# Normalised rows turned by transposing DMA on the sync queue instead of on TensorE

**Chip, cores, metric.** One core of one Trainium2 chip. The metric is the device time of one execution in microseconds (us), as the median of several runs. Runs are marked fast or slow by their state; only fast runs are compared.

## The reference

A block with two halves over 2048 rows of width 640. The first is an attention layer that works through segments of 32 rows, each preceded by 8 memory rows that are taken from the previous segment's own output, so the segments can't run side by side. The second is a feed-forward layer with a squared ReLU.

```python
def _A_ref(x, mem0, Wq, Wk, Wv, Wo, seg_len):
    mem = mem0
    for s in range(n_seg):                       # 64 segments, each needs the one before
        h = jnp.concatenate([mem, xs], axis=1)   # 8 memory rows + 32 rows of x
        q, k, v = (einsum('btd,dhe->bhte', h, W) for W in (Wq, Wk, Wv))   # 32 heads of 128
        p = _softmax(where(mask, q @ k * scale, -1e9))
        o = einsum('bhte,hed->btd', p @ v, Wo)
        mem = o[:, :M, :]
        outs.append(o[:, M:, :])

def _B_ref(x, w1, b1, w2, b2):                   # 640 -> 1728 -> 640
    r = relu(x @ w1 + b1)
    return (r * r) @ w2 + b2

h = x + _A_ref(_layernorm(x), ...)
return h + _B_ref(_layernorm(h), ...)
```

## The kernel before

The 64 segments are 16 blocks (128 rows each) of 4 steps. Between the pieces of a step's attention stand "fillers": units of the previous block's feed-forward and the tail projections of the next block. Rows are normalised in natural layout and then have to be turned, 128x640 in five 128x128 pieces, because the products that use them take them with the 640 along the partitions. Both turns are done on TensorE, with a copy out of PSUM on VectorE:

```python
def transposes(src):
    pt = mm.tile([128, DC, 128], BF16, tag="mm", name="pt")       # a bank of PSUM
    for c in range(DC):                                           # DC = 5
        nc.tensor.transpose(out=pt[:, c, :], in_=src(c), identity=ident)
    return pt

# norm_x: the rows of x, two blocks ahead
def turn():
    pt = transposes(lambda c: h["xn"][:, c * 128:(c + 1) * 128])
    ...
    def evac():                                                   # HT and hTt from pt, two copies
        nc.vector.tensor_copy(out=HT..., in_=pt[:, :, 0:96]...)
        nc.vector.tensor_copy(out=hTt[:], in_=pt[:, :, 96:128])
    late.append((0, evac))

# ffn: the rows that go into the feed-forward
def turn():
    pt = transposes(lambda c: h["hn"][:, c * 128:(c + 1) * 128])
    h["hnT"] = s1.tile([128, DC, 128], BF16, tag="hnT", name="hnT")
    late.append((0, lambda: nc.vector.tensor_copy(out=h["hnT"][:], in_=pt[:])))
    full.extend(...)                                              # its units may start
```

The turns are called in the middle of a step, ahead of the product O; `flush` first issues all the VectorE work that was put off. The end of a step is what the experiments turn on: SyncE issues the stores of the step's output rows (`keep`, "fo" in the profile), which wait for the copy `o`, and behind them the loads of feed-forward weights (`load_due`, "wf", 320 KB each, five buffers):

```python
def step(b, sp, fill):
    ...                                     # projections, scores, softmax sums, fillers
    if hturns:
        hturns.pop(0)()                     # step 2: the feed-forward's turn
    elif xturns:
        flush()                             # step 3: the turn of x
        xturns.pop(0)()
    pn = [normal(p[h], rz[h]) for h in range(2)]
    ...                                     # O, the copies oT, flush, fillers
    run_side()                              # parts of the normalising of later rows
    run_side()
    ...
    pw = bank(0, "pw")
    wo_units(lambda s: oT[s // 8][:, s % 8, TL:NQ], pw, slots_all)
    o = s2.tile([128, DG], BF16, tag="o", name="o")
    nc.scalar.copy(out=o[:], in_=pw[:, 0:DG])
    keep(o, b, sp * HD, M)                  # four stores on SyncE, they wait for o
    load_due()                              # three or four wf loads on SyncE
```

## Time and profile before

| | before |
|---|---|
| time | 1026.19 us, median of 3 (1025.86 to 1026.44) |
| span of the profiled run | 1027.4 us, mean granted clock 0.987 |
| TensorE busy | 952.6 us, 93% |
| VectorE / ScalarE / GpSimd busy | 516.3 / 434.8 / 161.3 us |
| step 3, blocks 2 to 14, in all | 198.9 us, TensorE idle for 12.8 of it |

Step lengths in this text are the distances between starts of the copy `o` from `pw` on ScalarE; there are 64 of them. A step runs from the copy of the step before it to its own copy, so fo and the wf loads that the program issues at the end of step 2 stand at the start of step 3 here. "Step 3" of a block is its fourth step. The prediction shows how the rest was read. Two lines of the waits view that it does not show are needed later (columns: engine, what waited, releaser; total us, times, longest us). The second is from the waits of SyncE's queue.

```profile
PE psf L355 <- DMA wf<-in_wf_dram: 3.4, 6, 1.1
```

```profile
SPq L300 <- ACT o L532: 282.1, 48, 12.0
```

TensorE waited little for feed-forward weights (psf is the feed-forward's "up" product). SyncE waited 282 us for the copies `o`: it had always got to the stores before the rows were there.

### The profile page before, as it was taken

How to read it: one execution, taken by the hardware profiler on the slowest of the kernel's cores; microseconds unless marked ns; L12 is line 12 of the kernel's file. 1: busy time of each engine (PE TensorE's matmuls, PEld its weight loads, DVE VectorE, ACT ScalarE, POOL GpSimd, SP SyncE). 2: the span in 40 equal slices, each digit the busy share in tenths (PEclk: the TensorE clock that was granted, in tenths of full speed). 3: DMA queues.
4: the chain of work that ended last, by engine and by line, in shares of the span. 5: the costliest groups of instructions: out<-in, count | busy, mean ns of one | idle time of the engine just before them, and what ended most of it. 6: DMA issues, size and time to landing. Idle time of an engine off the chain costs nothing.

```text
span 1027.4 us, 58454 instructions
## 1 busy us (share of the span) xinstructions
PE 952.6 (93%) x27584; PEld 624.4 (61%) x25755; DVE 516.3 (50%) x1362; ACT 434.8 (42%) x1084; POOL 161.3 (16%) x464
## 2 busy tenths in 40 slices
PE   2589889999999999999999999999999999999886
PEld 0155556666666756667675666667666666676454
DVE  2124355555645545564554556455555645555452
ACT  1144354444434443444445344444444444354331
POOL 0000101212120211212021121202112120301220
PEclk9979999999999999999999999999999999999998
DMA  9930002323422433242233424323342433234451
GB/s 352 423 143 22 19 16 70 105 87 102 129 76 83 118 107 102 86 129 82 80 116 105 125 64 129 101 86 90 106 126 64 129 102 94 75 112 121 152 174 63
DMA packets 74120, 114.70 MB, mean 112 GB/s; under 512 B 35344, under 2 KB 41616, under 8 KB 71440
## 3 DMA queue, kind: packets, MB, share of 16 engines
q1 hardware_dynamic: 73152, 110.60, 33.2%
q8 instruction: 208, 3.41, 1.4%
q10 hardware_dynamic: 720, 0.37, 0.1%
q14 instruction: 40, 0.33, 0.1%
HBM read 101.79 MB, written 6.55 MB: 105 GB/s over the span
## 4 chain that ended last, share of the span: by engine, by line
PE 84%; DMA 9%; DVE 3%; issue 2%; ACT 2%; POOL 1%; SPq 1%; POOLq 0%; DVEq 0%
PE ps L220 20%; PE ps L212 19%; PE pw L292 15%; PE pst L202 11%; PE psy L397 6%; PE psf L355 5%; DMA wf<-in_wf_dram 4%; PE pwt L292 3%; DMA wv<-in_wv_dram 2%; PE O L506 2%; DMA wk<-in_wk_dram 1%; DVE r L372 1%; PE pz L471 1%; PE A L457 1%; DMA wq<-in_wq_dram 1%
## 5 line engine op out<-in xcount | busy, mean ns | idle before, releaser
L428 ACT CAST row<-ps 128x512 bf16<-128x512 f32 x256 | 136.9, 586 | 153.4 <-PE ps L220 150.0
L220 PEld LDWEIGHTS <-HT 128*32 128x32 bf16 x3840 | 112.4, 97 | 120.3 <-issue 28.3
L292 PE MATMUL pw<-wo,oT 128*32 128x160 bf16 x8192 | 161.7, 237 | 10.4 <-issue 9.8
L292 PEld LDWEIGHTS <-oT 128*32 128x32 bf16 x8192 | 146.2, 99 | 34.7 <-ACT oT L517 20.8
L429 DVE STREAM_TRANSPOSE qT<-row 128x512 bf16<-128x512 bf16 x128 | 83.5, 690 | 128.5 <-ACT row L428 128.5
L212 PEld LDWEIGHTS <-HT 128*32 128x32 bf16 x2054 | 89.3, 97 | 73.0 <-issue 0.3
L220 PE MATMUL ps<-wq,HT 128*32 128x512 bf16 x1280 | 128.1, 381 | 0.8 <-DVE HT L195 0.8
L220 PE MATMUL ps<-wk,HT 128*32 128x512 bf16 x1280 | 128.0, 379 | 0.0
L212 PE MATMUL ps<-wk,HT 128*32 128x512 bf16 x1280 | 128.0, 379 | 0.0
L220 PE MATMUL ps<-wv,HT 128*32 128x512 bf16 x1280 | 127.7, 379 | 0.0
L212 PE MATMUL ps<-wv,HT 128*32 128x512 bf16 x1280 | 127.6, 379 | 0.0
L212 PE MATMUL ps<-wq,HT 128*32 128x512 bf16 x1280 | 127.4, 379 | 0.0
L520 POOL COPY oTt<-oT 128x64 bf16<-128x64 bf16 x256 | 49.5, 236 | 485.9 <-ACT oT L517 485.9
L429 DVE STREAM_TRANSPOSE kT<-row 128x512 bf16<-128x512 bf16 x128 | 83.5, 690 | 76.9 <-ACT row L428 76.9
L381 POOL TENSOR_TENSOR f1T<-r 128x256 bf16<-128x256 bf16 x93 | 57.7, 628 | 282.6 <-DVE r L372 131.5
L244 ACT CAST row<-pst 128x512 bf16<-128x512 f32 x96 | 56.2, 585 | 66.5 <-PE pst L202 56.9
L517 ACT CAST oT<-O 128x320 bf16<-128x320 f32 x128 | 48.3, 428 | 80.2 <-PE O L511 80.2
L202 PEld LDWEIGHTS <-hTt 128*32 128x32 bf16 x1920 | 47.4, 99 | 53.7 <-issue 29.9
L372 DVE TENSOR_SCALAR r<-psf,b1f 128x128 bf16<-128x128 f32 x218 | 66.2, 345 | 24.8 <-PE psf L355 15.9
L355 PE MATMUL psf<-hnT,wf 128*128 128x128 bf16 x1050 | 73.1, 219 | 5.1 <-DMA wf<-in_wf_dram 3.4
L532 ACT CAST o<-pw 128x160 bf16<-128x160 f32 x64 | 18.7, 292 | 137.0 <-PE pw L292 137.0
L519 DVE CAST oT<-O 128x320 bf16<-128x320 f32 x128 | 56.9, 486 | 39.1 <-PE O L511 39.1
(71 smaller groups left out, 1281.1 us busy)
## 6 DMA issues: line engine op xcount, KB each, us to landing
wf<-in_wf_dram SPq DMA_DIRECT2D x204, 320.0 KB
wq<-in_wq_dram SPq DMA_DIRECT2D x5, 1024.0 KB
wk<-in_wk_dram SPq DMA_DIRECT2D x5, 1024.0 KB
wv<-in_wv_dram SPq DMA_DIRECT2D x5, 1024.0 KB
wo<-in_wo_dram SPq DMA_DIRECT2D x4, 1280.0 KB
wq<-in_wf_dram SPq DMA_DIRECT2D x14, 320.0 KB
fo<-o SPq DMA_DIRECT2D x256, 7.5 KB
vturn<-row SPq DMA_DIRECT2D x120, 32.0 KB
```

The source lines that it names most:

```text
L202: nc.tensor.matmul(ps[32 * g:32 * g + 32, :], lhsT=lhs(c), rhs=w[:, c, g * EG + n * 512:g * EG + (n + 1) * 512], start=(c == 0), stop=(c = ...
L212: return te.add_instruction(mybir.InstMatmult(name=nc.get_next_instruction_name(), ins=[te.lower_ap(rhs), te.lower_ap(lhsT, for_matmul_wei ...
L220: (partial(again, g) if n else nc.tensor.matmul)(ps[n][32 * g:32 * g + 32, :], lhsT=lhs(c), rhs=w[:, c, g * EG + n * 512:g * EG + (n + 1) ...
L244: nc.scalar.copy(out=row[:], in_=st["ps"][:])
L292: nc.tensor.matmul(ps[32 * g:32 * g + 32, 0:DG], lhsT=lhs(s), rhs=wo[:, s, g * DG:(g + 1) * DG], start=(s == slots_all[0]), stop=(s == slo ...
L355: nc.tensor.matmul(ps[:, u * 128:(u + 1) * 128], lhsT=wfv[:, u, c], rhs=h["hnT"][:, c, :], start=(c == 0), stop=(c == DC - 1), skip_group_ ...
L372: nc.vector.tensor_scalar(out=r[0:fs, u, :], in0=src, scalar1=bias, scalar2=0.0, op0=ALU.add, op1=ALU.max)
L381: (nc.gpsimd if b < NB - 1 or k % 2 else nc.vector).tensor_tensor(out=f1T[:, 2 * k:2 * k + 2, :], in0=r[:], in1=r[:], op=ALU.mult)
L397: nc.tensor.matmul(h["ps"][:, 0:320], lhsT=f1T[:, fc + i, :], rhs=wf[:, (m % 4) * 320:(m % 4 + 1) * 320], start=(fc + i == 0), stop=(fc + ...
L428: nc.scalar.copy(out=row[:], in_=ps[n][:])
L429: nc.vector.transpose(out=dst(n), in_=blocks(row))
L519: nc.vector.tensor_copy(out=dst, in_=src)
```

## The change

The intent: take 145 turning instructions and the VectorE copies behind them off the busy engines, let idle SyncE and the DMA do the turn, and drop the flush ahead of O. The core of the diff (cut: the tile bookkeeping of the shared buffer `vrow`):

```diff
+    def turn_by_dma(out, src):
+        for c in range(DC):
+            nc.sync.dma_start_transpose(out=out[:, c, :], in_=src[:, c * 128:(c + 1) * 128])
+
 # norm_x
         def turn():
-            pt = transposes(lambda c: h["xn"][:, c * 128:(c + 1) * 128])
+            if b < 2:
+                pt = transposes(lambda c: h["xn"][:, c * 128:(c + 1) * 128])
+            else:
+                pt = s1.tile([128, DC, 128], BF16, tag="vrow", name="xT")
+                turn_by_dma(pt, h["xn"])
+            xturns.append(partial(spread, pt))
+
+        def spread(pt):
+            e = nc.vector if b < 2 else nc.gpsimd
...
+            e.tensor_copy(out=HT..., in_=pt[:, :, 0:96]...)
+            e.tensor_copy(out=hTt[:], in_=pt[:, :, 96:128])
...
-        return norm_steps(lambda: xt, dst, lambda: xturns.append(turn), order)
+        return norm_steps(lambda: xt, dst, turn, order)
 # ffn
         def turn():
-            pt = transposes(lambda c: h["hn"][:, c * 128:(c + 1) * 128])
             h["hnT"] = s1.tile([128, DC, 128], BF16, tag="hnT", name="hnT")
-            late.append((0, lambda: nc.vector.tensor_copy(out=h["hnT"][:], in_=pt[:])))
+            if b < NB - 1:
+                turn_by_dma(h["hnT"], h["hn"])
+            else:
+                ...                                   # last block: as before
+            hturns.append(ready)
 # step
         if hturns:
             hturns.pop(0)()
-        elif xturns:
-            flush()
-            xturns.pop(0)()
         pn = [normal(p[h], rz[h]) for h in range(2)]
...
         run_side()
         run_side()
+        if xturns:
+            xturns.pop(0)()
```

The transposes are now issued as soon as the rows are normalised, so they enter SyncE's queue there, ahead of whatever the program puts into it later.

More of the change, by code (lines that the diff above doesn't have):

```diff
@@ L177, in turn @@
             HTs[b], hTts[b] = HT, hTt
-            def evac():
-                nc.vector.tensor_copy(out=HT[:, 0:DC * 128].rearrange("p (c s r) -> p c s r", c=DC, s=4)[:, :, :, M:SEG],
-                                      in_=pt[:, :, 0:96].rearrange("p c (s r) -> p c s r", s=4))
-                nc.vector.tensor_copy(out=hTt[:], in_=pt[:, :, 96:128])
-            late.append((0, evac))
+            e.tensor_copy(out=HT[:, 0:DC * 128].rearrange("p (c s r) -> p c s r", c=DC, s=4)[:, :, :, M:SEG],
+                          in_=pt[:, :, 0:96].rearrange("p c (s r) -> p c s r", s=4))
+            e.tensor_copy(out=hTt[:], in_=pt[:, :, 96:128])
         def order(ap, i=0):
@@ L206, in blocks @@
     def blocks(row):
-        return row[:].rearrange("p (b r) -> p b r", r=32)
+        return row.rearrange("p (b r) -> p b r", r=32)
     def again(g, out, lhsT, rhs, start, stop):
@@ L242, in put @@
         def put(n):
-            row = (s1 if which == "v" and b else s3).tile([128, 512], BF16, tag="vrow" if which == "v" and b else "row", name="row")
-            nc.scalar.copy(out=row[:], in_=st["ps"][:])
+            if which == "v" and b:
+                row = s1.tile([128, D], BF16, tag="vrow", name="vrow")[:, 0:512]
+            else:
+                row = s3.tile([128, 512], BF16, tag="row", name="row")[:]
+            nc.scalar.copy(out=row, in_=st["ps"][:])
             if which == "q":
-                nc.vector.transpose(out=t[:, n * 512:(n + 1) * 512], in_=row[:])
+                nc.vector.transpose(out=t[:, n * 512:(n + 1) * 512], in_=row)
             elif which == "k":
@@ L340, in turn, with ready @@
         def turn():
-            pt = transposes(lambda c: h["hn"][:, c * 128:(c + 1) * 128])
             h["hnT"] = s1.tile([128, DC, 128], BF16, tag="hnT", name="hnT")
-            late.append((0, lambda: nc.vector.tensor_copy(out=h["hnT"][:], in_=pt[:])))
+            if b < NB - 1:
+                turn_by_dma(h["hnT"], h["hn"])
+            else:
+                pt = transposes(lambda c: h["hn"][:, c * 128:(c + 1) * 128])
+                late.append((0, lambda: nc.vector.tensor_copy(out=h["hnT"][:], in_=pt[:])))
+            hturns.append(ready)
+        def ready():
             full.extend((up(n // 2, n % 2), n == 0) for n in range(FC))
@@ L408, in down @@
             return f
-        return [loads, add] + norm_steps(lambda: h["h"], dst, lambda: hturns.append(turn))
+        return [loads, add] + norm_steps(lambda: h["h"], dst, turn)
     def step(b, sp, fill):
@@ L428, in step @@
                 nc.scalar.copy(out=row[:], in_=ps[n][:])
-                nc.vector.transpose(out=dst(n), in_=blocks(row))
+                nc.vector.transpose(out=dst(n), in_=blocks(row[:]))
             run_side()
```

## The prediction

> **What bounds the kernel now.** I read the page first (busy times, chain by line), then the timeline of one whole block, the windows view of one stretch in all four of its steps, the chain in order of time for one step, and the queue of SyncE.
>
> ```profile
> PE 952.6 (93%) x27584; PEld 624.4 (61%) x25755; DVE 516.3 (50%) x1362; ACT 434.8 (42%) x1084; POOL 161.3 (16%) x464
> PE 84%; DMA 9%; DVE 3%; issue 2%; ACT 2%; POOL 1%; SPq 1%; POOLq 0%; DVEq 0%
> L162 PE MATMUL pt<-cs,xn 128*128 128x128 bf16 x160 | 15.0, 227 | 11.7 <-DVE xn L151 11.7
> L343 DVE COPY hnT<-pt 128x640 bf16<-128x640 bf16 x16 | 7.7, 482 | 0.5 <-PE pt L162 0.4
> L180 DVE COPY HT<-pt 128x480 bf16<-128x480 bf16 x16 | 6.4, 399 | 1.6 <-PE pt L162 1.6
> ```
>
> TensorE is the bound: 93% busy and 84% of the chain. The transposes are 160 of its instructions and 15.0 us of its busy time (0.47 us per turn of five), and they start from DVE copies that are a small part of a half-idle engine. So what can be saved is about 1.5% in TensorE time, plus whatever the turns make TensorE wait for.
>
> The program is 16 blocks of 4 steps. I cut it at the starts of the copy of the memory rows (o from pw on ScalarE, 64 of them). From block 2 to 13 the undisturbed steps repeat to 0.02 us: step 0 takes 15.95, step 1 13.57, step 2 13.97, step 3 14.91 us, and single steps are longer by named waits. The feed-forward turn stands in step 2, the turn of x in step 3. The windows view of block 13, from the first score load to the first tail projection after O, for steps 1, 2, 3 and for step 0 of the same block (durations are the second column):
>
> ```profile
> 844.56:848.00 3.44, 3.44 (x114) 2.42 (x107) 1.38 (x5) 2.37 (x7) 0.00 (x0) 1.00 0.85 269
> 858.25:861.97 3.72, 3.72 (x121) 2.79 (x113) 1.91 (x7) 2.37 (x7) 0.00 (x0) 1.00 0.41 120
> 872.09:876.92 4.83, 4.13 (x141) 3.58 (x132) 4.04 (x13) 2.37 (x7) 1.95 (x3) 1.00 0.80 258
> 830.92:834.43 3.51, 3.51 (x135) 3.13 (x126) 2.43 (x10) 2.37 (x7) 0.61 (x1) 1.00 0.04 11
> ```
>
> Steps 1 and 2 do the same work there except for the turn: 0.28 us. Steps 0 and 3 both do seven "up" units; step 3 is 1.32 us longer, TensorE is idle for 0.70 of it, and VectorE is busy for 4.04 instead of 2.43. Its chain says why:
>
> ```profile
> 873.79 0.62 DVE r L372 x2
> 874.55 0.62 POOL f1T L381
> 875.19 0.61 DVE r L372 x2
> 875.80 0.15 DVE pn L481
> 876.21 0.53 DVE pn L482
> 876.78 0.21 PE O L511 x4
> ```
>
> The five transposes of x (875.11 to 875.48 in the timeline) are not in that chain at all. The turn of x comes with a flush, which puts all six r evictions, and their wait for a GpSimd square, ahead of the pn products that O needs. The last pn takes 0.60 us and not 0.18, beside a GpSimd square. In step 3 the flush costs, not the transposes.
>
> **What the Trainium skill says.** "VectorE: DVE Perf Modes", The three transpose paths: 390 ns for a 128x128 bf16 turn on TensorE into PSUM, 1309 ns by the DMA crossbar into SBUF. The trace has 219 ns as the median of one transpose, and 0.28 to 0.47 us for five pipelined ones, so the page's TensorE figure is far too high for this use; no DMA transpose is in the trace. "DMA: Bandwidth & Descriptors", DMA Transpose (X-bar): only the hardware queues may issue it, and into SBUF; Rules for kernel authors there adds that a transpose next to ordinary DMAs needs nothing. No run shows it yet. "GPSIMD Engine Reference", specification table: it shares SBUF interfaces with VectorE, in contention with two-input instructions; the 0.60 against 0.18 us above agrees. "Runtime: NRT & Kernel Launch", Instruction fetch mechanics: instructions come in blocks of 256 by the engine's own DMA queue. The trace agrees in size: 208 instruction packets for 3.41 MB, 16.4 KB each.
>
> **The change, part by part.**
> *Removed from TensorE.* 14 x turns (blocks 2 to 15) and 15 feed-forward turns (0 to 14): 145 transposes, 145 weight loads. In step 2 that is worth the measured 0.28 us: 13 blocks x 0.28 = 3.6 us. In block 15 the hnT turn before the scores' fillers cost a wait of 0.58 us and some 0.35 us of transposes: 0.9 us if the DMA is in time.
> *Removed with it, the flush.* Step 3 of block 14 has up units but no turn of x, hence no flush: 14.32 us, 0.53 of it a wait for wf, so 13.79 net. Against 14.91 that is 1.12 us. Steps 3 of blocks 1 to 13 add up to 199.4 us; 13 x 13.79 = 179.3; the difference of 20.1 holds 3.8 us of "issue" stalls inside pw and 2.8 us of wf waits, which stay: 13.5 us to be had. Six of these steps (blocks 2, 3, 6, 7, 10, 12) have the issue stall, 0.22 to 1.03 us, some 100 TensorE instructions into pw. I take it for an instruction block that has not arrived, asked for before O; whatever is saved between the asking and there only lengthens the stall. I take off half of 6 x 1.12: 3 us. About 10.5 us stay. Block 0, whose step 3 waits for pn anyway, adds some 0.3.
> *Kept weight loads.* The kernel keeps redundant loads to steer where pw begins within 256 instructions. Counted by step they are 15, 60, 50, 13. Ten instructions fewer in steps 2 and 3 make it 60 and 23, within the 60 available, and cost nothing: step 1 with 60 and step 3 with 13 both take 7.00 us from the cut to the scores.
> *VectorE.* 15 x 0.48 + 14 x 0.63 = 16 us of copies go; they stand beside pw, off the path. *GpSimd* gets two copies per x turn. It copies 64 elements in 236 ns and 256 in 400 ns, which gives an estimate of some 0.6 + 0.3 = 0.9 us, 13 us in all, on an engine 16% busy. It comes after the oT copies and the squares of its step, and the next block needs it a step later: hidden.
> *SyncE and the DMA.* The five transposes wait for the normalised rows, then land. For step 2 of block 13 (columns: start, duration):
>
> ```profile
> 856.45 2.50 SPq L271 DMA_DIRECT2D vturn<-row  x4
> 863.57 0.35 SPq L407 DMA_DIRECT2D out_dram<-fx  x1
> 865.41 3.14 SPq L300 DMA_DIRECT2D fo<-o  x4
> 868.66 2.41 SPq L102 DMA_DIRECT2D wf<-in_wf_dram  x4
> ```
>
> The rows are ready at 858.9, so SyncE has 6.5 us before it must issue fo, and the wf loads behind it. An ordinary issue takes 0.35 to 0.8 us here. Five transposes take 2 to 4 us at that rate, or 6.5 if each holds the queue for the page's 1309 ns: it just fits. hnT is first read at 872.8, 14 us after the rows; xT must be there by the next step's middle. With 6.5 us plus a landing of about 2 (my guess), both are in time.
> *Sum.* 3.6 + 0.9 + 10.5 + 0.3 = 15.3 us. Against it I set 3 us for wf loads that come later or weight and instruction fetches that share the DMA engines with the transposes: in step 3 wf is just in time already (waits of 0.22 to 1.07 us in five of these blocks). 1026.2 - 12.3 = about 1014 us.
>
> **The rivals.**
> 1. *SyncE or the DMA becomes the bound.* If a transpose holds the queue or its rings for more than 1.3 us, fo and then wf are late by 5T - 6.5 us in step 3 of each block. At T = 2 us that is 3.5 x 14 = 49 us, less the 15 gained: about 1060 us. For: wf is on the edge already and SyncE works through a backlog of 6 to 7 us at the start of each step. Against: the queue is idle in just these stretches, 4.5 us before out_dram and 5 us before fo in step 3.
> 2. *All the slack is gained.* The instruction stalls go with the changed DMA traffic and wf is no later: 3.6 + 0.9 + 0.3 + 13.5 + 3.8 = 22 us, 1004 us. For: in blocks 8, 9, 11, 13 neither stall shows. Against: the same loads of x, and now the transposes, run while that fetch is under way.
> 3. *The wait moves.* With the turn gone, O waits for pn or for instructions instead and only the flush's part or less is gained: 6 to 8 us, 1019 us. For: in blocks 0 and 1 the turn only fills a wait for pn. Against: steps 0 and 1 reach O without any such wait.
>
> **Range and chances.** The centre is 1014. The low end, 1001, is rival 2 with a little more; the high end, 1031, is a transpose of about 1.55 us on the queue, which eats the gain (5 x 1.55 - 6.5 = 1.25 us in 14 blocks). A gain of over 2% needs 1006 or less, that is nearly everything of rival 2: 0.14. A loss of over 2% needs transposes of about 1.8 us or slower: 0.11. Within 2%: 0.75.
>
> **What would show it.** Right: no L162 in blocks 2 to 14; step 2 at about 13.7 us; the scores-to-tail stretch of step 3 at about 3.5 us with r evictions after oT; kept loads 15, 60, 60, 23; six step-3 stalls in pw still there, longer; VectorE about 16 us less busy, GpSimd 13 more; five transposes issued within 6 us. Wrong: wf waits of over 1 us in most blocks, SyncE's fo issues late against the o copy, psf waiting for a DMA hnT, the next block's tail projection waiting for GpSimd's HT, or "issue" stalls in steps that had none.

## The result

The changed kernel took **1060.59 us** (median of 4 runs, 1052.20 to 1069.28; the longest was in the slow state), the kernel before 1026.03 us in the same rounds (4 runs). The ratio is **1.0318** (95% interval 1.0239 to 1.0397): slower, where "within 2%" was predicted. Here and below a ratio is the mean time of one kernel's fast runs over that of the other's of the same rounds, so not quite the ratio of the medians quoted.

Step lengths from the two traces, in us (median of blocks 2 to 13, and the sum over all 16 blocks):

| | step 0 | step 1 | step 2 | step 3 |
|---|---|---|---|---|
| before, median | 15.99 | 13.57 | 13.97 | 15.24 |
| after, median | 15.97 | 13.75 | 13.69 | **19.04** |
| before, sum | 308.2 | 225.3 | 225.2 | 243.8 |
| after, sum | 305.6 | 224.1 | 220.8 | **287.4** |

(The median of 15.24 before holds the named waits; undisturbed it is 14.91.) Everything except step 3 is as before or better, but for 0.2 us in the median of step 1. Two lines of the page of the changed kernel (busy times, and the chain by engine), and its group of "up" products (busy us, mean ns, idle time before, releaser):

```profile
PE 962.6 (91%) x27439; PEld 623.7 (59%) x25890; DVE 497.1 (47%) x1319; ACT 435.3 (41%) x1084; POOL 170.5 (16%) x492
...
PE 81%; DMA 15%; ACT 2%; SPq 1%; issue 1%; DVE 1%; DVEq 0%
...
L374 PE MATMUL psf<-hnT,wf 128*128 128x128 bf16 x1050 | 81.4, 225 | 42.9 <-DMA wf<-in_wf_dram 41.2
```

TensorE has 145 instructions fewer and is busy for 10 us *more*: a first sign that its clock was lower. The share of DMA in the chain rose from 9% to 15%, and 41.2 of the 42.9 us before the "up" products are waits for weights. The waits of TensorE and of SyncE's queue say the same:

```profile
PE psf L374 <- DMA wf<-in_wf_dram: 41.2, 32, 3.7
```

```profile
SPq L313 <- ACT o L550: 193.4, 37, 11.2
```

SyncE found the rows `o` not yet ready only 37 times instead of 48, and waited 89 us less for them: in the other steps it came late. Its queue from step 2 into step 3 of block 13 (start, duration) shows why (the profile calls the normalised rows xn in both halves). The copy `o` that opens step 3 was made at 896.13:

```profile
890.21 7.99 SPq L167 DMA_TRANSPOSE hnT<-xn  x5
898.30 0.52 SPq L426 DMA_DIRECT2D out_dram<-fx  x1
898.92 3.23 SPq L313 DMA_DIRECT2D fo<-o  x4
902.26 1.87 SPq L102 DMA_DIRECT2D wf<-in_wf_dram  x4
...
906.10 7.37 SPq L167 DMA_TRANSPOSE xT<-xn  x5
```

Five transposing DMAs hold the queue for 7.99 us. Of the 145, 98 take less than 1.3 us (the median is 1.23) and 47 take 1.5 to 2.6 us, with 0.04 us between one and the next (median); five take 7.84 us in step 2 and 7.24 us in step 3 (medians). So fo is issued 2.8 us after the copy instead of 0.3, and wf behind it. From the issue records and the DMA packets of blocks 2 to 13 (medians, us from the start of step 3):

| | feed-forward transposes end | first fo | first wf issued | last wf landed |
|---|---|---|---|---|
| before | – | 0.32 | 3.56 | 10.5 |
| after | 2.07 | 2.79 | 6.69 | 14.1 |

The last weights land 3.6 us later, in a step that is meant to last 13.6. The second part of the loss is the clock. In step 3 of block 2, TensorE waited 3.72 us for the last wf (timeline of TensorE; in brackets the idle time before):

```profile
222.33 0.72 PE L374 MATMUL psf<-hnT,wf 128*128 128x128 bf16 x5 [3.72 <-DMA wf<-in_wf_dram]
```

The windows view around it (columns: window, length, busy us and instructions of PE, PEld, DVE, ACT, POOL, then granted clock, DMA share, GB/s):

```profile
217.00:219.00 2.00, 1.46 (x20) 1.12 (x20) 0.48 (x4) 0.35 (x2) 0.00 (x0) 1.00 1.00 354
219.00:221.00 2.00, 0.00 (x0) 0.00 (x0) 0.00 (x0) 0.00 (x0) 0.00 (x0) 0.97 0.62 167
221.00:223.00 2.00, 0.67 (x9) 0.48 (x13) 0.00 (x0) 0.00 (x0) 0.00 (x0) 0.50 0.07 22
223.00:225.00 2.00, 2.00 (x65) 1.12 (x68) 1.29 (x4) 0.76 (x3) 0.89 (x5) 0.50 0.17 38
```

After the wait the granted clock is 0.50 for more than 4 us, in the middle of O and pw. The Trainium skill has this: "TensorE: Matmul & The Clock Gate", What's actually happening, gives half clock after an idle window of about 3.4 us and a free-running window of 3413 ns. The trace agrees on the period: the clock records change at multiples of 3.413 us. On how much idle time it takes it does not (see the last section). Between blocks 2 and 14 there are nine spells of half clock, of 3.41 or 6.83 us each, with 41.1 us of TensorE work in them. The kernel before has none there.

This gives a ledger of step 3, blocks 2 to 14. The reference point is the changed kernel with its wf loads issued earlier (early_wf below), where the wait is gone:

| us | in all | TensorE idle | TensorE busy | busy at half clock |
|---|---|---|---|---|
| before | 198.9 | 12.8 | 186.1 | 0 |
| after | 242.2 | 40.6 | 201.6 | 41.1 |
| after, wf loads early | 177.8 | 0.2 | 177.6 | 0 |

Of the 64.4 us between the second and third rows, 40.4 are idle time and 24.0 longer work. TensorE's 27439 instructions are the same in both kernels, so the two traces can be compared one by one: those that began at half clock took 41.8 us, and the same ones 23.0 us in early_wf. That is 18.8 us for the clock; the other 5 us are not explained here. The change saves 21.1 us in these steps and loses 64.4.

### The profile page after: what moved, and what is told of

The parts are those of the page before. It is cut to its first block, busy times and chain, and to the rows that moved or that the text cites. A ratio compares the mean times of both kernels' runs of the same rounds, so it can differ in the third digit from the quotient of the medians.

```text
span 1062.4 us, 58677 instructions
## 1 busy us (share of the span) xinstructions
PE 962.6 (91%) x27439; PEld 623.7 (59%) x25890; DVE 497.1 (47%) x1319; ACT 435.3 (41%) x1084; POOL 170.5 (16%) x492
## 3 DMA queue, kind: packets, MB, share of 16 engines
q8 instruction: 208, 3.41, 1.3%
## 4 chain that ended last, share of the span: by engine, by line
PE 81%; DMA 15%; ACT 2%; SPq 1%; issue 1%; DVE 1%; DVEq 0%
PE ps L230 19%; PE ps L222 18%; PE pw L305 14%; DMA wf<-in_wf_dram 11%; PE pst L212 11%; PE psy L416 5%; PE psf L374 4%; PE pwt L305 3%; PE O L522 2%; DMA wv<-in_wv_dram 2%; DMA wk<-in_wk_dram 1%; PE pz L490 1%; PE A L476 1%; DMA wq<-in_wq_dram 1%; PE A L471 1%
## 5 line engine op out<-in xcount | busy, mean ns | idle before, releaser
L305 PE MATMUL pw<-wo,oT 128*32 128x160 bf16 x8192 | 167.5, 243 | 6.4 <-issue 5.6
L305 PEld LDWEIGHTS <-oT 128*32 128x32 bf16 x8192 | 154.2, 102 | 31.9 <-ACT oT L533 21.7
L230 PE MATMUL ps<-wk,HT 128*32 128x512 bf16 x1280 | 126.6, 379 | 0.0
L222 PE MATMUL ps<-wk,HT 128*32 128x512 bf16 x1280 | 126.6, 379 | 0.0
L374 PE MATMUL psf<-hnT,wf 128*128 128x128 bf16 x1050 | 81.4, 225 | 42.9 <-DMA wf<-in_wf_dram 41.2
L374 PEld LDWEIGHTS <-wf 128*128 128x128 bf16 x1050 | 62.0, 100 | 55.3 <-DMA wf<-in_wf_dram 49.5
```

The costliest lines, as they stand in the source:

```text
L222: return te.add_instruction(mybir.InstMatmult(name=nc.get_next_instruction_name(), ins=[te.lower_ap(rhs), te.lower_ap(lhsT, for_matmul_wei ...
L230: (partial(again, g) if n else nc.tensor.matmul)(ps[n][32 * g:32 * g + 32, :], lhsT=lhs(c), rhs=w[:, c, g * EG + n * 512:g * EG + (n + 1) ...
L305: nc.tensor.matmul(ps[32 * g:32 * g + 32, 0:DG], lhsT=lhs(s), rhs=wo[:, s, g * DG:(g + 1) * DG], start=(s == slots_all[0]), stop=(s == slo ...
L374: nc.tensor.matmul(ps[:, u * 128:(u + 1) * 128], lhsT=wfv[:, u, c], rhs=h["hnT"][:, c, :], start=(c == 0), stop=(c == DC - 1), skip_group_ ...
```

## The experiments

Theory A: SyncE's time. The five transposes hold SyncE's queue, so fo and wf are issued late, and wf was on the edge. Rival B: what is in flight (the transposes of x in step 3 share the DMA rings with wf, or slow them down). Rival C: the transposes themselves are not needed for the gain; the flush was what cost. Rival D, added later: a transposing DMA does something besides holding the queue. All fifteen runs gave correct results. Step lengths are medians of blocks 2 to 13 in the profiled run.

| kernel | median us (range, runs) | ratio to before (95%) | step 0 | 1 | 2 | 3 |
|---|---|---|---|---|---|---|
| h_only | 1066.56 (1055.88–1078.01, 4) | none given | 15.95 | 13.91 | 13.69 | 18.35 |
| x_only | 1025.21 (1017.92–1032.72, 12) | 1.0012 (0.9984–1.0041) | 16.55 | 13.61 | 13.97 | 14.66 |
| early_wf | 1004.64 (1003.71–1007.30, 4) | 0.9813 (0.9779–0.9847) | 16.70 | 13.57 | 13.90 | 13.61 |
| one_call | 1015.00 (1011.86–1019.10, 8) | 0.9911 (0.9879–0.9943) | 15.98 | 13.93 | 13.69 | 14.88 |
| one_call_early_wf | 1016.98 (1013.00–1017.77, 6) | 0.9946 (0.9930–0.9962) | 17.42 | 13.78 | 13.69 | 13.67 |
| before_early_wf | 1019.75 (1014.82–1024.95, 20) | 0.9951 (0.9931–0.9970) | 15.95 | 13.84 | 13.97 | 14.91 |
| before_no_flush | 1031.09 (1028.04–1040.75, 4) | 1.0101 (1.0038–1.0163) | 15.98 | 14.18 | 13.97 | 15.47 |
| before_no_flush_early_wf | 1019.14 (1012.83–1021.59, 16) | 0.9932 (0.9907–0.9956) | 16.00 | 13.65 | 13.97 | 14.82 |
| before_sync_held | 1025.77 (1022.51–1031.85, 8) | 1.0035 (0.9995–1.0075) | 15.95 | 13.92 | 13.97 | 15.13 |
| five_early_2 | 1066.20 (1062.22–1071.56, 4) | 1.0445 (1.0401–1.0489) | 21.60 | 13.57 | 13.69 | 13.64 |
| one_call_early_2 | 997.29 (996.99–1001.57, 4) | 0.9780 (0.9741–0.9818) | 16.07 | 13.88 | 13.69 | 13.70 |
| one_call_early_not3 | 1003.08 (996.53–1004.47, 4) | 0.9811 (0.9769–0.9853) | 16.21 | 13.57 | 13.69 | 13.78 |
| before_sync_held_long | 1073.66 (1071.85–1086.41, 4) | 1.0508 (1.0441–1.0575) | 15.95 | 13.82 | 13.97 | 19.34 |
| before_early_2 | 1016.69 (1013.47–1020.45, 8) | 0.9924 (0.9894–0.9954) | 15.95 | 13.66 | 13.97 | 14.91 |
| one_call_early_2_again | 1000.61 (998.59–1005.63, 6) | 0.9764 (0.9729–0.9799) | 16.08 | 13.66 | 13.69 | 13.63 |

The kernels ran in four groups, in the order of the table: four, four, four and three. The kernel before had medians of 1023.87, 1024.78, 1021.26 and 1025.00 us in their rounds.

### One turn at a time: h_only and x_only

h_only is the changed kernel with the turn of x put back on TensorE, with its flush. x_only has the feed-forward's turn put back. Abridged:

```diff
 # h_only (norm_x; and the call with its flush ahead of O, as before)
         def turn():
-            if b < 2: ... else: turn_by_dma(pt, h["xn"])
+            pt = transposes(lambda c: h["xn"][:, c * 128:(c + 1) * 128])
 # x_only (ffn)
         def turn():
+            pt = transposes(lambda c: h["hn"][:, c * 128:(c + 1) * 128])
             h["hnT"] = s1.tile([128, DC, 128], BF16, tag="hnT", name="hnT")
-            turn_by_dma(h["hnT"], h["hn"])
+            late.append((0, lambda: nc.vector.tensor_copy(out=h["hnT"][:], in_=pt[:])))
```

> Only the feed-forward rows are turned by DMA; x as before, with its flush. Theory A (the five hnT transposes hold SyncE for some 8 us in step 2, so fo and the wf loads behind it are issued 2 to 3 us late, and TensorE waits for wf in step 3): all of the wf waits stay, 30 to 45 us in sum, and since the flush's 1.1 us per block is not gained the time is about as after or longer, 1050 to 1075 us. Rival B (the xT transposes of step 3 sit in the DMA rings with the wf loads still in flight and draw out their landing): the wf waits go back to under 12 us and the time is 1018 to 1028 us.

> Only the rows of x are turned by DMA, and the flush is gone; the feed-forward rows are turned by TensorE as before. Theory A: SyncE is free in step 2, wf is on time, step 3 takes about 13.8 us where no wf wait stands; 1006 to 1016 us. Rival B: long wf waits in step 3 as after, 1045 to 1060 us.

h_only has the loss: its two fast runs took 1055.88 and 1058.05 us (the other two were in the slow state, and no ratio was given), step 3 is 18.35 us, psf waits 35.8 us for wf. It has no transposing DMA of x at all, and those of the feed-forward end 2.4 us into step 3 (median), before the first wf is issued at 6.8. x_only, which has transposes in step 3, waits 4.9 us for wf and is as fast as before. Rival B falls: it is the transposes of *step 2* that make step 3 long, through what stands behind them in the queue.

x_only missed what I expected, some 1% gain. In its steps 3 of blocks 2 to 14 stand 6.7 us of instruction stalls inside pw ("issue", 7 times; 3.8 us in 6 before) and 4.9 us of waits for wf (7 times; 3.4 us in 6 before). That is what the prediction feared of the time saved ahead of O: part of it lengthens the wait for whatever comes next. Its step 0 is 16.55 us instead of 15.99, too; there the transposes of x delay fo to 2.29 us, but no wait of TensorE over 0.3 us goes with it, and the cause stays open.

### The queue's order: early_wf

```diff
+        load_due()                 # ahead of pw, so ahead of the stores of o
         pw = bank(0, "pw")
```

> The changed kernel with the wf loads put on the SyncE queue before the memory rows' writes (fo) instead of behind them; both turns by DMA as after. Theory A: wf is issued some 3.5 us earlier in step 2, the wf waits fall under 10 us, 1000 to 1012 us. Rival B: the wf loads now meet the hnT transposes in the rings, or still the xT ones, and the waits stay over 25 us, 1040 us or more.

The transposes still hold the queue for 7.8 us, but wf is now issued before fo, from 2.69 us into step 3 (median) instead of 6.69. Step 3 falls from 19.04 to 13.61 us, psf waits 2.2 us in all, the half-clock spells are gone, and the kernel takes 1004.64 us. This is what theory A says. (Its step 0 is 16.70 us instead of 15.97; the loads are early in every step here. What stretches step 0 in this kernel was not found.)

### Fewer instructions for the same turn: one_call

```diff
     def turn_by_dma(out, src):
-        for c in range(DC):
-            nc.sync.dma_start_transpose(out=out[:, c, :], in_=src[:, c * 128:(c + 1) * 128])
+        nc.sync.dma_start_transpose(out=out[:], in_=src[:])
```

> One transposing DMA of the whole 128x640 per turn instead of five of 128x128. If the 1.5 us hold of SyncE is a cost of each instruction, the turn takes 1.5 to 3 us of SyncE and theory A gives 1004 to 1015 us; if it is a cost of each tile moved, the turn still takes about 7 to 8 us and the time stays at 1050 to 1065 us. Rival B expects 1045 us or more in either case, as the same bytes go through the rings.

SyncE's queue, step 2 into step 3 of block 13 (step 3 begins at 854.82):

```profile
849.51 2.08 SPq L166 DMA_TRANSPOSE hnT<-xn  x1
853.64 0.36 SPq L425 DMA_DIRECT2D out_dram<-fx  x1
855.13 3.15 SPq L312 DMA_DIRECT2D fo<-o  x4
858.39 2.19 SPq L102 DMA_DIRECT2D wf<-in_wf_dram  x4
...
862.57 1.25 SPq L166 DMA_TRANSPOSE xT<-xn  x1
```

One instruction for 128x640 holds the queue for 1.25 us (median of both kinds; the 2.08 here is one of seven that took 1.98 to 2.27). That is as long as one for 128x128 does. The hold is a price per instruction, not per tile. fo is on time (0.32 us into the step), and the kernel is 0.9% faster than before. Stalls inside pw (7.1 us in the steps 3 of blocks 2 to 14) and waits for wf (6.6 us) keep step 3 at 14.88.

### Both together: one_call_early_wf

```diff
 # one_call
+        load_due()
         pw = bank(0, "pw")
```

> Both mends at once: one transposing DMA per turn, and the wf loads ahead of the memory rows' writes. If SyncE's time was all that was wrong, the wf waits of all steps stay under 5 us, step 3 takes 13.6 us and step 0 goes back from the 16.7 us of the early_wf run to 16.0: 994 to 1002 us. If the stretched step 0 there came from something else (the DMA rings, instruction fetches), it stays and the time is that of early_wf, 1002 to 1007.

A miss: 1016.98 us, no better than one_call. Step 3 is now 13.67 us and no wf wait is left, but step 0 went from 15.98 to 17.42. TensorE's instruction blocks are fetched by DMA (208 packets of 16.4 KB in the trace before), and in one_call a block is fetched 0.5 us before step 0 begins (median). With the wf loads of the step before moving data from -1.3 to +3.3 us, that fetch starts at 0 to +2.0 us instead, and pwt (the tail's output product) waits for instructions 15 times, 18.1 us in all (one_call: 3.7; of these 3.8 and 3.3 us stand at the very end of both kernels). Weights that come early where nobody needs them early push the instructions out.

### The same on the kernel before: before_early_wf, before_no_flush, before_no_flush_early_wf

```diff
 # before_early_wf and before_no_flush_early_wf
+        load_due()
         pw = bank(0, "pw")
 # both no_flush kernels
-        elif xturns:
-            flush()
-            xturns.pop(0)()
         pn = [normal(p[h], rz[h]) for h in range(2)]
...
         run_side()
+        if xturns:
+            xturns.pop(0)()
+            flush()
```

> The kernel before, with TensorE's turns and the flush, and only the wf loads put ahead of the memory rows' writes: how much of the early_wf gain has nothing to do with the DMA turn. Its wf waits of some 7 us and part of its stalls in pw go: 1008 to 1018 us. Theory that early wf only repairs what the DMA turn broke: 1020 to 1026 us.

> The kernel before with all turns on TensorE, only the turn of x moved behind the oT copies so that no flush stands ahead of pn. My prediction put 1.1 us per step 3 down to the flush and not to the transposes: step 3 at about 14.2 us (13.8 and the transposes' 0.4) where nothing else waits, 1010 to 1017 us. If the transposes themselves were the cost, step 3 stays at 14.9 us and the time at 1020 to 1026.

> No DMA turn at all, no flush, wf early: what the two mends that need no transposing DMA reach. Against one_call_early_wf this gives the worth of the DMA turn itself: if it is the 145 transposes' TensorE time (0.28 us in step 2 and about 0.4 in step 3 of each block), this kernel takes 1002 to 1010 us and is 8 to 10 us longer than one_call_early_wf; if it is nothing, both are equal within 3 us.

before_early_wf gains 0.5%: wf waits vanish, and step 3 keeps its 14.91 us. Early weights alone are not the gain of early_wf.

before_no_flush tests the prediction's claim that the flush costs and the transposes do not. TensorE still turns x, but behind the copies oT, with no flush ahead of O. I expected a gain and got 1031.09 us. With early weights as well (to take the wf waits out of the picture) it takes 1019.14, and step 3 is 14.82, not 13.7. The timeline of TensorE in step 3 of block 8, and the waits of the tile pt (us, times):

```profile
571.75 0.44 PE L162 MATMUL pt<-cs,xn 128*128 128x128 bf16 x5 [0.69 <-ACT row L244]
```

```profile
ACT row L244: 9.2, 13
```

At the new place the turn waits for a PSUM buffer that ScalarE still has to empty, 9.2 / 13 = 0.71 us each time, and then takes 0.44 us itself: about what separates 14.82 from 13.77, the length of step 3 of block 14, which has no turn. So neither place tried for this turn on TensorE is cheap: ahead of O it costs the flush, behind oT a PSUM buffer. Rival C falls as it was put. The flush did cost, but it was not to be had for nothing with the turn on TensorE.

### SyncE's time without a transposing DMA: before_sync_held and before_sync_held_long

The kernel before, with plain small stores (24x160 elements to scratch memory that nothing reads) put to SyncE where the feed-forward's rows are normalised.

```diff
+        def hold():
+            hturns.append(turn)
+            if b < NB - 1:
+                spare = dram.tile([10, 24, DG], BF16, tag="hold", name="hold")
+                for i in range(10):                  # before_sync_held_long: 17
+                    nc.sync.dma_start(out=spare[i], in_=h["hn"][0:24, 0:DG])
```

> The kernel before, all turns on TensorE and the flush kept, plus ten small ordinary DMAs (24 rows of 320 bytes, to a scratch that nobody reads) at the place where the changed kernel issues the five hnT transposes. They hold SyncE for an estimated 10 x 0.75 = 7.5 us, as long as the transposes do, and move 77 KB without the crossbar. If SyncE's time alone is the cause, step 3 shows the wf waits of the h_only run, 25 us or more in sum, and the time is 1045 to 1070 us. If the crossbar's hold on the DMA engines is needed for the loss, the waits stay under 12 us and the time is 1024 to 1035.

> The kernel before with 17 small stores instead of 10 where the feed-forward's rows are normalised, so that SyncE is held for about 7.8 us (17 x 0.46 us, measured with 10), as long as the five transposes hold it, with no transposing DMA in the program and TensorE's work unchanged. Theory A (SyncE's time alone): fo and the wf loads of step 3 are issued 2 to 3.5 us late, waits of psf for wf come to 25 to 45 us in all, step 3 grows from 14.9 to 17.5 to 19.5 us, about 1060 us (1048 to 1075). Rival D (a transposing DMA does something besides holding the queue, so that a hold by other transfers is harmless): step 3 stays under 15.5 us, below 1035 us.

With 10 stores nothing happened (ratio 1.0035), but the dose was too small: 4.0 to 6.5 us in blocks 2 to 13, over 0.75 us before step 3 begins (median), so fo was on time in most blocks. In two of the four blocks where it was 0.8 to 1.2 us late, step 3 took 17.9 and 16.25 us. Inconclusive.

With 17 stores the hold is about as long as that of the five transposes, a little longer (median 8.4 us; it ends 2.6 us into step 3 instead of 2.1). Its queue at step 3 of block 13 (begins at 899.52), and TensorE's wait:

```profile
893.87 8.14 SPq L415 DMA_DIRECT2D hold<-xn  x17
902.12 0.36 SPq L407 DMA_DIRECT2D out_dram<-fx  x1
902.58 3.15 SPq L300 DMA_DIRECT2D fo<-o  x4
905.84 1.87 SPq L102 DMA_DIRECT2D wf<-in_wf_dram  x4
```

```profile
PE psf L355 <- DMA wf<-in_wf_dram: 40.6, 22, 4.6
```

wf is first issued 6.76 us into step 3 (changed kernel 6.69) and last lands at 13.9 (14.1); psf waits 40.6 us (41.2); step 3 takes 19.34 us (19.04); 47.5 us of TensorE work fall into half clock (41.1). The loss is there in full without a single transposing DMA. Theory A is shown, and rival D is not needed. It is 13 us slower than the changed kernel (in other rounds); the turns on TensorE and their flush are still in it, which was not tested apart.

### Early weights only where they are needed: five_early_2, one_call_early_2, one_call_early_not3

```diff
 # five_early_2: on the changed kernel; one_call_early_2: on one_call
+        if sp == 2:                # one_call_early_not3: if sp != 3
+            load_due()
         pw = bank(0, "pw")
```

> The changed kernel with five DMAs per turn, and the wf loads moved ahead of the fo writes in step 2 alone. If the late wf issue of step 2 is the whole loss, step 3 takes 13.6 to 14.2 us and nothing else changes: 998 to 1006 us, with step 0 at 16.0 us, without the stretch that early_wf had there. If early_wf gained in other steps, 1010 us or more.

> One DMA per turn, wf ahead of fo in step 2 alone. In one_call_early_wf an instruction fetch due at the start of step 0 met wf loads in flight (late fetches, 0.3 to 2.2 us of issue stalls in the tail of wo); here the loads of step 3 go back behind fo. Step 0 then takes 16.0 us, step 3 13.6 us: 995 to 1003 us. If the stretch of step 0 had another cause, 1010 us or more.

> As one_call_early_2, but wf ahead of fo in steps 0, 1 and 2: step 1 should lose its wf waits (13.6 instead of 13.9 us) without the stretch in step 0. 993 to 1001 us, 2 to 4 us under one_call_early_2; if early loads meet instruction fetches in steps 1 and 2 too, it is the slower of the two.

five_early_2 missed badly: 1066.20 us where I expected about 1002. Step 3 is mended (13.64), but step 0 takes 21.60. Its queue in step 3 of block 13 (begins at 899.68) and into the next step 0:

```profile
893.80 7.59 SPq L167 DMA_TRANSPOSE hnT<-xn  x5
...
902.11 2.81 SPq L102 DMA_DIRECT2D wf<-in_wf_dram  x4
905.01 3.17 SPq L313 DMA_DIRECT2D fo<-o  x4
...
911.31 7.87 SPq L167 DMA_TRANSPOSE xT<-xn  x5
...
920.25 3.09 SPq L313 DMA_DIRECT2D fo<-o  x4
923.45 1.39 SPq L102 DMA_DIRECT2D wf<-in_wf_dram  x3
```

The five transposes of x now run over the end of the shorter step 3; fo and wf of step 0 are 6.9 and 7.5 us later than before (0.32 to 7.18 and 3.47 to 10.93, medians). In the changed kernel the 19 us of step 3 had hidden this. The wait moved one step on, which is theory A again, in a place I had not looked at.

one_call_early_2 shortens both holds to one instruction and puts the weights early only in step 2: 997.29 us, ratio 0.9780. Step 3 is 13.70, TensorE is idle for 0.4 us in the 13 steps 3 of blocks 2 to 14, and the stalls in pw and pwt are 3.8 and 2.7 us. one_call_early_not3 gets step 1 down too (13.57) but stalls more inside pw (7.2 us), and comes out no better.

### Does it hold, and what is the change's part: before_early_2 and one_call_early_2_again

before_early_2 is the kernel before with the same three lines; one_call_early_2_again is the same kernel as one_call_early_2, on another chip.

> The kernel before, TensorE still turning, with the wf loads of step 2 alone put to the queue ahead of pw. It asks how much of the best version's gain is the queue's order and how much the change. If the order is most of it: 1003 to 1010 us. If, as I think, the change is most of it (its 1.2 us of step 3 and 0.28 us of step 2 are only there with the transposes off TensorE): waits for wf fall under 2 us, step 3 stays at 14.9 us, step 2 at 13.97, 1016 to 1023 us.

> The same kernel as one_call_early_2, again, with five rounds on what may be another chip: does a ratio of 0.978 to the kernel before hold? Expected 0.974 to 0.983, 996 to 1003 us, step 3 at 13.7 us. If the first result was luck of the instruction fetches, the ratio lies above 0.985.

The result holds: ratio 0.9764 (0.9729 to 0.9799). Its page:

```profile
PE 940.8 (94%) x27439; PEld 610.1 (61%) x25890; DVE 497.5 (50%) x1319; ACT 434.7 (44%) x1084; POOL 169.9 (17%) x492
```

Against the changed kernel, TensorE does the same 27439 instructions in 940.8 us instead of 962.6: most of that is the clock, by the ledger above. The queue's order alone gives 0.8% on the kernel before, the turn in one call alone 0.9%, both together 2.2 to 2.4%, a little more than the sum. A reason for that, argued and not tested: early weights have no 13.7 us step to serve while TensorE turns x (step 3 stays at 14.91), and the turn in one call loses part of its gain to stalls inside pw and waits for wf while wf comes late.

## Why the prediction was wrong

**The step that failed** is "6.5 if each holds the queue for the page's 1309 ns: it just fits", in the paragraph on SyncE and the DMA, and with it the use of the ordinary issue rate ("2 to 4 us at that rate"). I compared the wrong two numbers and left no margin:

- *Size of the hold.* Five took 7.84 us, not 2 to 6.5. Most of them take 1.23 us, near the skill's 1309 ns; but a third take 1.5 to 2.6 us, so T in the formula is 7.84 / 5 = 1.57 us. By that formula, 5T - 6.5, wf should be 1.3 us late.
- *What stands between.* It was 3.1 us late (3.56 to 6.69). The hold began 5.6 us before the step, 6.0 and not 6.5 before fo was due, out_dram comes behind it, and fo itself then took longer to get through. A budget of "time until the next issue" has to count every issue that is in between.
- *What lateness costs.* I charged a late wf at its lateness. The range's high end, 1031, was a transpose of about 1.55 us, which is what was measured; the time was 1060. Being 3.1 us late lengthened step 3 by 5.4 us against a clean 13.61, because TensorE's waits (40.4 us over 13 steps, 3.1 each) brought half clock with them. That factor was nowhere in the prediction. The rival's formula gave about 1060 only for T = 2 us; it named the right mechanism and arrives at the right time by errors that cancel: T too large, the issues in between left out, the clock left out, the gain too small.
- *The odds.* "The queue is idle in just these stretches" was true, but it was idle because it waited for `o`: that idle time was the margin, and I spent it as if it were free. (Two readings there were off without harm: in step 3 the queue idled 6.1 to 7.9 us before fo, not 5, and the five transposes of x end at 875.55, not 875.48.)

**What was right.** Step 2 fell to 13.69 us (predicted 13.7). The kept weight loads are 15, 60, 60 and 23. No L162 is left in blocks 2 to 14. VectorE is 19 us less busy (predicted 16), GpSimd 9 us more (13); its two copies take 585 and 322 ns (estimated 0.6 and 0.3 us). The spread on GpSimd makes TensorE wait nowhere in the changed kernel. The landing that I guessed at about 2 us took 3.3 (median from issue), still in time. TensorE never waits for a transposed hnT in blocks 0 to 14. Step 2 of block 15 fell from 16.41 to 13.88 us, more than the 0.9 I gave it.

**The gain in step 3** was there and was larger than I booked. I had found 20.1 us to be had and took 10.5. With the queue in order (one_call_early_2), steps 3 of blocks 2 to 14 fall from 198.9 to 178.5 us: 20.4. That is the second rival, whose 1004 us the best version passes. "In step 3 the flush costs, not the transposes" was half right, as before_no_flush_early_wf shows.

**The stalls inside pw.** "Still there, longer" was right for x_only and one_call (12.6 and 14.6 us in the whole kernel against 9.8 before), where fo and wf of step 3 were issued on time. In the changed kernel itself they were 5.6 us, of which 0.4 in these steps 3: I suppose that the long waits for wf gave the instructions time to come, which no run tests.

**What stays open.** Why the last of a wf load's 16 completions comes up to 3.5 us behind the others in some steps (block 2: fifteen by 218.8, the last at 222.28). It happens in before_sync_held_long too, up to 2.2 us and without a transposing DMA in the program, so it isn't theirs alone; beyond that no run settles it. Nor was the half clock tested by itself: it follows the waits in every trace that has it, and goes when the waits go, but its 18.8 us come from comparing two traces and not from a run of its own.

## What to carry to other kernels

An idle queue that stands waiting for data is not free time: before moving work to it, add up every issue between the new work and the next one that something depends on, and look one step further for the place where the wait will come out next. Issue one large transposing DMA and not five small ones; here the hold is a price per instruction. When waits on TensorE add up to some 1.7 us within 3.4, reckon with more than the waits: here its clock was then halved for 3.4 or 6.8 us behind them.

## What the Trainium skill lacked or had wrong

- **The hold of a transposing DMA on its issuing engine.** "VectorE: DVE Perf Modes", The three transpose paths, has 1309 ns for 128x128, which reads as the time of the turn. The runs show 1.23 us of SyncE per instruction (median; 47 of 145 took 1.5 to 2.6), 7.84 us for five, and 1.25 us for one of 128x640: a price of the issue, which the page does not say. "DMA: Bandwidth & Descriptors", DMA Transpose (X-bar), has the constraints but no such cost; elsewhere that page has sequencer cycles of transposing DMAs of other sizes, in a section on a newer chip.
- **Issue time.** "DMA: Bandwidth & Descriptors", Issuing engines are not separate DMA queues, calls the sequencer's time to start a DMA "usually small relative to the DMA itself". Here it decided the time: 17 stores of 24x160 elements held SyncE for 8.14 us and cost 5% of the kernel (before_sync_held_long), with little data moved.
- **How short an idle time halves the clock.** "TensorE: Matmul & The Clock Gate", HAM oscillation, puts the rule at no idle gaps over about 3.4 us. In step 3 of the changed kernel a longest idle time of 1.77 us (block 4) and a first one of 1.79 us (block 7) were each followed by a clock of 0.50 within about a microsecond, while one of 1.60 us (block 13) was not. What tells them apart in these traces is the idle time of TensorE summed over the 3.413-us period of the clock records that has just ended. In the seventeen traces, blocks 2 to 14, it was 1.68 us or more, about half of the period, before each of the 38 falls; of 3756 full-clock periods without a fall behind them, four had as much (1.71 to 1.97 us).
- **Instruction fetch.** "Runtime: NRT & Kernel Launch", Instruction fetch mechanics, calls the crossing of a block "mostly hidden". With weight loads in flight when a block is asked for (one_call_early_wf), TensorE stalled inside pwt in step 0 of each of the blocks 2 to 15, 14.3 us in all and up to 2.2 us at once; in one_call these steps have 0.5 us.
- **TensorE's transpose.** The 390 ns of "VectorE: DVE Perf Modes", The three transpose paths, for a 128x128 turn are too many for pipelined use ("TensorE: Matmul & The Clock Gate", PE-mode transpose, calls that figure one in isolation and has about 275 ns within a kernel): 219 ns for one and 0.44 us for five in a row (step 3 of before_no_flush_early_wf).
